# Ten of sixteen final blocks get x added in place by transfers that POOL issues, with a fourth place for the Gram copies and a new table of priorities

## The chip, the core and the metric

The kernel runs on one core of a Trainium2 chip. Five engines work side by side, each through its own list of instructions in order: TensorE (PE in the profile, with PEld for its weight loads), VectorE (DVE), ScalarE (ACT), GpSimd (POOL), and SyncE (SP), which here issues the transfers between DRAM and on-chip memory. The metric is the device time of one execution in microseconds (us); the time before is the median of 3 runs.

## The reference

x has 2048 tokens of 512 features in float32. After a layer norm, two branches are computed from the same xn and joined at the end:

```
xn = layernorm(x)
q, k, v = split_heads(xn @ wqkv)                       # 32 heads of 16
phi(t) = where(t > 0, t + 1, exp(t)) + 1e-6
kv = phi(k)^T @ v      z = sum over tokens of phi(k)   # per head
s  = (phi(q) @ kv / (phi(q) @ z + 1e-6)) @ wo
g  = silu((gelu(xn @ w_gate) * (xn @ w_up)) @ w_down)  # 512 -> 1792 -> 512
out = x + s * g
```

## The kernel before, in words

**Products.** A float32 factor is split into a high part of reduced precision and a low remainder (`split`: ACT casts the high part, DVE subtracts it). Each product is then three matmuls, high by high, high by low and low by high (`sum3`). The large products are Strassen products of two-by-two blocks, seven instead of eight (`PRODUCTS`); POOL forms sums of blocks for them, and ACT and DVE split these.

**Stages.** Tokens are worked on in blocks of 128. First x is loaded, normalized and transposed, k and q are computed, and a Gram matrix of phi(k) and xn is gathered over all tokens in four banks of PSUM, `gps`. Then comes the feed-forward branch in two passes of 1024 tokens (p = 1, then p = 0), each with units of w_gate, w_up and w_down, whose prepared forms go to DRAM in the first pass and come back in the second. The banks of gate and up products are called FX, FY, FZ, those of the down products DX, DY, DZ. The sums of the down products stand in eight tiles `acc`, for p = 1 also stored to DRAM (`g1_d`) and loaded again as `g1_0` to `g1_7` for the final stage, so that the space can be used between.

**Gram copies.** After its last matmul each `gps` bank is copied to a tile `GTa` and stored to `g_d`. Two copies are made by ACT, two by DVE. The tiles come from a ring of three places in the pool `up`, shared with other tiles of tag "p", so that the later copies wait until a store of an earlier one has landed. Places of this pool are used again by the first gate values `g` of the feed-forward branch.

**Final stage.** `s_forms` loads the normalized queries from DRAM in blocks (`pb`, `wide`) and makes the Strassen forms: Xh, Xl for p = 1, and sf0h, sf0l, sf1h, sf1l for p = 0. `s_quad(p, c, ...)` then makes seven products in four PSUM banks SX, SY, SZ, SV, and `block(dh, th, ...)` finishes each output block of 128 x 512. There are sixteen, by p, k = 2·dh + c and th. A block multiplies s by silu(g) and adds x. The way is A (product into PSUM by DVE), B (product into the g or acc tile by DVE) or C (DVE saves the sum, POOL multiplies). The add of x then is one more instruction, on POOL for the blocks in `ON_POOL` and else on DVE; it adds into a tile `xp` that `x_again` loaded with x before. SP stores the result: for p = 1 one store of 512 KB for every pair of blocks, for p = 0 one of 256 KB for every block. The very last block, `LAST`, is done in two halves.

**Layout.** s comes out with 32-column pieces of its 512 columns in another order than g. The views `turned` and `by_turn` rearrange while they read, and x and the output are laid out on the host in this turned order for all blocks.

**Order.** Nothing is written in program order. `do` records each operation with an engine and a cost, `Plan.order` plays a list scheduler over them with the numbers in `PRIORITY` (one for each operation, the smallest first among those that are ready), and each engine's list is what comes out. So a change of any number can move work on all five lists.

Of the kernel before, what the change touches and what calls it, by code (L numbers as in the profile page):

```python
# [40 lines left out]

PRIORITY = """
# [1497 lines left out]
```

## Time and profile before

| | us |
|---|---|
| three runs | 595.03, 593.09, 595.22 (median 595.03) |
| the profiled execution, own time | 594.95 |
| its span, first to last instruction | 593.0 |
| around the span | 1.95 |
| PE busy | 583.7 (98%) |
| DVE busy | 484.0 (82%) |
| POOL busy | 345.4 (58%) |
| ACT busy | 323.4 (55%) |
| mean DMA rate | 250 GB/s |

A row of the timeline gives start, duration, engine, source line, operation, tiles and count; in brackets behind it the idle time ahead and what ended it. Matmuls overlap: one of 128x512 is drawn 0.39 us long, while the next one starts 0.227 us after it. So a lost stretch of PE is the distance of two starts less 0.227, and the idle time that a row shows is some 0.16 us less than the loss. For a transfer the view of DMA issues gives the size and the median time from issue to landing.

### The profile page before, as it was taken

How to read it: one execution, taken by the hardware profiler on the slowest of the kernel's cores; microseconds unless marked ns; L12 is line 12 of the kernel's file. 1: busy time of each engine (PE TensorE's matmuls, PEld its weight loads, DVE VectorE, ACT ScalarE, POOL GpSimd, SP SyncE). 2: the span in 40 equal slices, each digit the busy share in tenths (PEclk: the TensorE clock that was granted, in tenths of full speed). 3: DMA queues.
4: the chain of work that ended last, by engine and by line, in shares of the span. 5: the costliest groups of instructions: out<-in, count | busy, mean ns of one | idle time of the engine just before them, and what ended most of it. 6: DMA issues, size and time to landing. Idle time of an engine off the chain costs nothing.

```text
span 593.0 us, 8082 instructions
## 1 busy us (share of the span) xinstructions
PE 583.7 (98%) x2588; PEld 478.7 (81%) x2588; DVE 484.0 (82%) x729; ACT 323.4 (55%) x588; POOL 345.4 (58%) x291
## 2 busy tenths in 40 slices
PE   9999999999999999999999999999999999999996
PEld 7888888887888888888888878888788888887774
DVE  6999888984788987899888975777458887779997
ACT  6766778775766654575454325434325531457741
POOL 3503586325796966879588325356335652666776
PEclk9999999999999999999999999999999999999999
DMA  7157775556958766974659999699759977899725
GB/s 253 50 177 222 239 244 157 169 177 223 355 185 273 247 208 207 341 267 160 219 175 378 374 330 342 179 321 289 266 203 360 408 260 226 264 328 340 257 109 224
DMA packets 80969, 148.37 MB, mean 250 GB/s; under 512 B 18592, under 2 KB 34208, under 8 KB 80928
## 3 DMA queue, kind: packets, MB, share of 16 engines
q1 hardware_dynamic: 80928, 147.87, 72.9%
q8 instruction: 20, 0.33, 0.2%
q14 instruction: 21, 0.17, 0.1%
HBM read 83.62 MB, written 64.23 MB: 249 GB/s over the span
## 4 chain that ended last, share of the span: by engine, by line
PE 89%; DVE 5%; DMA 4%; ACT 1%; SPq 0%; issue 0%; POOL 0%; DVEq 0%; ACTq 0%
PE FX L573 25%; PE DX L573 12%; PE FZ L573 12%; PE gps L573 7%; PE DZ L573 6%; PE FY L573 6%; PE X L573 6%; PE DY L573 3%; PE Z L573 3%; PE q L573 2%; PE k L573 2%; PE Y L573 1%; DMA w<-w_d 1%; PE SX L573 1%; DVE Xl L554 1%; DMA xp0h<-in_xt 1%
## 5 line engine op out<-in xcount | busy, mean ns | idle before, releaser
L573 PE MATMUL FX<-Xh,w 128*128 128x512 f32 x448 | 152.0, 389 | 0.4 <-DMA w<-w_d 0.4
L1140 POOL TENSOR_TENSOR h<-h,g 128x512 f32<-128x512 f32 x42 | 63.2, 1506 | 76.4 <-DVE h L554 61.1
L573 PEld LDWEIGHTS FX<-Xh,w 128*128 128x128 f32 x448 | 84.0, 188 | 18.2 <-ACT fu L548 0.8
L554 POOL TENSOR_TENSOR h<-h,h 128x512 f32<-128x512 f32 x56 | 83.5, 1490 | 19.2 <-DVE hf3l L554 4.2
L573 PE MATMUL FX<-Xl,w 128*128 128x512 f32 x224 | 87.2, 389 | 0.0
L573 PE MATMUL FZ<-Xh,w 128*128 128x512 f32 x224 | 77.4, 389 | 0.0
L548 ACT COPY fu<-FX 128x512 f32<-128x512 f32 x56 | 32.9, 588 | 57.4 <-PE FX L573 43.9
L573 PE MATMUL gps<-pks,xns 128*128 128x512 f32 x192 | 50.3, 392 | 0.0
L573 PEld LDWEIGHTS FZ<-Xh,w 128*128 128x128 f32 x224 | 42.0, 188 | 8.8
L573 PEld LDWEIGHTS FX<-Xl,w 128*128 128x128 f32 x224 | 42.0, 188 | 8.7
L554 POOL TENSOR_TENSOR wide<-wide 128x256 f32<-128x256 f32 (+1 forms) x38 | 38.6, 1027 | 14.4 <-DVE m L554 6.5
L1166 DVE TENSOR_TENSOR acc<-acc,DX 128x512 f32<-128x512 f32 x48 | 32.4, 682 | 16.0 <-PE DX L573 15.8
L573 PE MATMUL FZ<-Xl,w 128*128 128x512 f32 x112 | 43.6, 389 | 0.0
L557 POOL TENSOR_TENSOR zacc<-zacc,kp 128x512 f32<-128x512 f32 x16 | 24.6, 1536 | 30.9 <-DVE kp L849 28.0
L573 PEld LDWEIGHTS gps<-pks,xns 128*128 128x128 f32 x192 | 35.7, 188 | 7.3
L573 PE MATMUL FY<-Xh,w 128*128 128x512 f32 x112 | 39.2, 391 | 0.8 <-DVE g L554 0.8
L1132 ACT ACTIVATE g<-g 128x512 f32<-128x512 f32 x42 | 26.6, 633 | 19.9 <-DVE g L554 19.7
L554 POOL TENSOR_TENSOR wide<-q,zacc 128x512 f32<-128x512 f32 x16 | 21.3, 1354 | 21.6 <-DMA q<-q_d 12.1
L554 DVE TENSOR_TENSOR g<-fu,FZ 128x512 f32<-128x512 f32 x28 | 19.1, 682 | 15.9 <-PE FZ L573 9.1
L573 PE MATMUL X<-kq,Xh 128*128 128x512 f32 x96 | 31.2, 393 | 0.0
L548 ACT COPY fe<-FX 128x512 f32<-128x512 f32 x28 | 16.5, 588 | 26.1 <-PE FX L573 18.9
L1166 DVE TENSOR_TENSOR acc<-acc,DZ 128x512 f32<-128x512 f32 x32 | 21.7, 683 | 8.6 <-PE DZ L573 8.5
(377 smaller groups left out, 1537.7 us busy)
## 6 DMA issues: line engine op xcount, KB each, us to landing
w_d<-w SPq DMA_DIRECT2D x36, 512.0 KB, 4.7
w<-w_d SPq DMA_DIRECT2D x36, 512.0 KB, 6.2
wd_d<-wd SPq DMA_DIRECT2D x21, 512.0 KB, 4.7
wd<-wd_d SPq DMA_DIRECT2D x21, 512.0 KB, 5.6
x<-in_first SPq DMA_DIRECT2D x16, 256.0 KB, 3.0
q_d<-qp SPq DMA_DIRECT2D x16, 256.0 KB, 2.2
q<-q_d SPq DMA_DIRECT2D x16, 256.0 KB, 5.0
pn_d<-wide SPq DMA_DIRECT2D x16, 256.0 KB, 5.5
```

The costliest lines, as they stand in the source:

```text
L548: do("ACT", act(n), lambda o, i: nc.scalar.copy(o, i), dst, src, name=name)
L554: do(eng, c, lambda o, p, q: getattr(e, f"tensor_{op}")(o, p, q), dst, a, b, name=name)
L557: do("POOL", pool(D), lambda o, i: nc.gpsimd.tensor_add(o, o, i), dst, src, name=name)
L573: nc.tensor.matmul(o, v[i], v[i + 1], start=start and part == 0 and i == 0, stop=stop and part == 1 and i == len(v) - 2, skip_group_check=on)
L1132: curved("gelu", do("ACT", curve(NC), lambda o, i: nc.scalar.activation(o, i, AF.Gelu_apprx_tanh), g, ps if e is None else g, name="gelu"))
L1140: do("POOL", pool(NC), lambda o, i: nc.gpsimd.tensor_mul(o, o, i), h, g, name="h")
L1166: do("DVE", dve(NC), lambda o, i: nc.vector.tensor_add(o, o, i), a, ps, name="acc")
```

## The change

- Ten of the sixteen blocks (all eight of p = 1, and (k, th) = (0, 0) and (2, 1) of p = 0) are listed in `NATURAL`. For them the product goes into the g or acc tile (way A becomes B), and then x is added to that tile by a transfer from DRAM which accumulates, issued by POOL (`gained`). The tile is then stored from there by SP. The separate add, and the `xp` tile of p = 1 with its four loads of 512 KB, are gone; for p = 0 six loads of 256 KB take the place of four of 512 KB. The ten blocks are stored one by one, in the tile's own layout; the host lays x and the output out accordingly.
- `ON_POOL` keeps four blocks of p = 0. By the built lists DVE makes seven adds fewer and one more (block (0, 1) of the last quad, before on POOL), and POOL makes four adds fewer (two of p = 1, two of p = 0) and ten issues more.
- The Gram copies have a ring of their own with four places.
- `sf1` of p = 0 is made from tiles `pb` in places of the ring `BR` that `xp` used before, no longer from `wide`.
- All numbers of `PRIORITY` are other numbers.

```
+NATURAL = {(p, k, th) for p in range(2) for k in range(4) for th in range(2) if p or (k, th) in ((0, 0), (2, 1))}
 PRIORITY = """
-113295 113257 110076 102616 117147 119271 0 2123 110187 109121 111695 111606 111697 111790 116707 118955 118027 116257 75973 94787 75934 94720 91206
...
+173791 176819 174775 169344 169336 176625 174707 169786 173425
 """
...
+    def gained(dst, src):
+        op = do("POOL", 0.9, lambda o, i: nc.gpsimd.dma_start(o, i, accum_op=ALU.add), dst, src, name="xg")
+        op.port, op.land = False, 4.0
...
     for c in range(KT):
-        g = U("p", range(18, 21), f"GTa{c}")
+        g = U("gt", [18, 19, 20, 14], f"GTa{c}")
         copy("DVE" if c % 2 else "ACT", g, gps[c], D, "GT")
         dma(g_d(c, (slice(None), c)), g, 256, "store")
...
-    ON_POOL = ((3, 0, 1), (0, 0, 1), (1, 0, 0), (2, 0, 1), (2, 1, 0), (2, 1, 1), (3, 0, 0), (3, 1, 1))
+    ON_POOL = ((2, 0, 1), (2, 1, 0), (3, 0, 0), (3, 1, 1))
...
         def block(dh, th, e, ps, to):
-            v, o = g[dh, c, th], xp[2 * dh + c]
+            v, o = g[dh, c, th], xp.get(2 * dh + c)
             how = WAYS.get((n, dh, th), "A")
             k = 2 * dh + c
+            natural = (p, k, th) in NATURAL
+            if natural and how == "A":
+                how = "B"
...
+            if natural:
+                gained(v, ext(xt[p, k, th]))
+                dma(ext(out[k * P:(k + 1) * P, p * HALF + th * NC:][:, :NC]), v, 256, "store")
+                return
...
-                if not p:
-                    dma(ext(out[k * P:(k + 1) * P, lo:lo + w]), x, w // 2, "store")
-            if p:
-                left[k] = left.get(k, 2) - 1
-                if not left[k]:
-                    dma(ext(out[k * P:(k + 1) * P, HALF:2 * HALF]), o, 512, "store")
+                dma(ext(out[k * P:(k + 1) * P, lo:lo + w]), x, w // 2, "store")
...
-    def x_again(p):
+    def x_again():
         got = {}
-        whole = {} if p else {hl: tile_in("xf", f"{hl}0", [P, 2, HALF], F32, f"xp0{hl}", 2) for hl in "hl"}
-        for k in (0, 2, 1, 3):
-            got[k] = tile_in("dp", ring("br", BR), [P, HALF], F32, f"xp{p}{k}", 4) if p else whole["hl"[k // 2]].part(
-                [Res() for _ in range(4)], (slice(None), k % 2))
-            dma(got[k].map(lambda ap: ap.rearrange("p (h c) -> p h c", h=2)), ext(xt[p, k].rearrange("h p c -> p h c")), 512, "first")
+        for c, hl in enumerate("hl"):
+            whole = tile_in("xf", f"{hl}0", [P, 2, HALF], F32, f"xp{c}", 2)
+            for k in (c, c + 2):
+                got[k] = whole.part([Res() for _ in range(4)], (slice(None), k // 2))
+                for th in range(2):
+                    if (0, k, th) not in NATURAL:
+                        dma(got[k].part(got[k].res[2 * th:2 * th + 2], (slice(None), slice(th * NC, (th + 1) * NC))), ext(xt[0, k, th]), 256, "first")
         return got
```

How the lists move is shown at three places, by rows of the built programs: line, operation, tiles with their numbers, size, and the semaphores waited for. A semaphore named for an engine counts that engine's work. DMAHW0 to DMAHW7 count the landings of SP's transfers, which take the eight in turn; DMASW0 to DMASW7 do so for POOL's.

**The Gram copies, on DVE.** Before, at the end of the last `gps` matmuls; `w12` and `w13` are weight forms, `g11_0` is the first gate value, which frees the bank FY:

```order
L554 TENSOR_TENSOR w00_1609<-raw0_859,w00_1609 128x512 [waits Activation_49]
L554 TENSOR_TENSOR w12_1635<-w1tmp_1623,w12_1635 128x512 [waits Activation_49]
L554 TENSOR_TENSOR w13_1651<-w1tmp_1623,w13_1651 128x512 [waits Activation_49]
L550 COPY GTa3_1672<-gps3_435 128x512 [waits DMAHW6_49,DMAHW1_49,PE_49]
L554 TENSOR_TENSOR g11_0_1680<-fe1_0_1658,FY0_1617 128x512 [waits DMAHW5_49,DMAHW2_49,Activation_49]
L554 TENSOR_TENSOR wd00_1668<-wide_206,wd00_1668 128x512 [waits Activation_49]
```

and now:

```order
L555 TENSOR_TENSOR w00_1609<-raw0_859,w00_1609 128x512 [waits Activation_49]
L551 COPY GTa1_1627<-gps1_382 128x512 [waits DMAHW5_49,PE_49]
L555 TENSOR_TENSOR w12_1643<-w1tmp_1622,w12_1643 128x512 [waits Activation_49]
L555 TENSOR_TENSOR w13_1654<-w1tmp_1622,w13_1654 128x512 [waits Activation_49]
L551 COPY GTa3_1672<-gps3_379 128x512 [waits DVE_49,PE_49]
L555 TENSOR_TENSOR g11_0_1684<-fe1_0_1676,FY0_1634 128x512 [waits DMAHW0_49,DVE_49,Activation_49]
L555 TENSOR_TENSOR wd00_1665<-wide_206,wd00_1665 128x512
```

The copy of `gps1` stands ahead of `w12` now, and the copy of `gps3` waits for no transfer; `g11_0` waits for DMAHW0, on which the store of `GTa1` lands.

**Loads of weights in the second pass, on SP.** Before (`g1_d` rows store acc tiles, `w100` and `w102` are gate weights of the next unit):

```order
L523 DMA g1_d_92<-acc1_5_2006 128x512 [waits DMAHW3_49,DVE_49]
L523 DMA wd53_3514<-wd53_d_165 128x1024 [waits DMAHW4_49,PE_49]
L523 DMA wd63_3520<-wd63_d_169 128x1024 [waits DMAHW5_49,PE_49]
L523 DMA g1_d_92<-acc1_3_1983 128x512 [waits DMAHW6_49,DVE_49]
L523 DMA g1_d_92<-acc1_1_1977 128x512 [waits DMAHW7_49,DVE_49]
L523 DMA g1_d_92<-acc1_7_2019 128x512 [waits DMAHW0_49,DVE_49]
L523 DMA w100_3538<-w100_d_154 128x1024 [waits DMAHW1_49,PE_49]
L523 DMA w102_3550<-w102_d_156 128x1024 [waits DMAHW2_49,PE_49]
```

and now:

```order
L524 DMA g1_d_92<-acc1_1_1967 128x512 [waits DMAHW3_49,DVE_49]
L524 DMA wd53_3513<-wd53_d_165 128x1024 [waits DMAHW4_49,PE_49]
L524 DMA g1_d_92<-acc1_3_2002 128x512 [waits DMAHW5_49,DVE_49]
L524 DMA w102_3522<-w102_d_156 128x1024 [waits DMAHW6_49,PE_49]
L524 DMA wd63_3530<-wd63_d_169 128x1024 [waits DMAHW7_49,PE_49]
L524 DMA g1_d_92<-acc1_5_1998 128x512 [waits DMAHW0_49,DVE_49]
L524 DMA w100_3543<-w100_d_154 128x1024 [waits DMAHW1_49,PE_49]
L524 DMA g1_d_92<-acc1_7_2023 128x512 [waits DMAHW2_49,DVE_49]
```

`w102` stands ahead of two of the stores of acc tiles now, `w100` ahead of one.

**The final stage, on POOL and DVE.** POOL before, from the first sum for the forms of p = 0 to the first add of p = 0:

```order
L554 TENSOR_TENSOR pb000_5290<-pb001_5349,pb000_5290 128x512 [waits DMAHW3_49,Pool_49]
L554 TENSOR_TENSOR g1_2_5263<-g1_2_5263,se1_1_5423 128x4x4x32 [waits DVE_49]
L554 TENSOR_TENSOR pb001_5349<-pb001_5349,pb000_5290 128x512 [waits DVE_49,Activation_49,Pool_49]
L554 TENSOR_TENSOR pb001_5349<-pb001_5349 128x512 [waits DMAHW4_49,Pool_49]
L554 TENSOR_TENSOR wide_206<-wide_206 128x512 [waits DMAHW6_49,DMAHW0_49,DVE_49]
L554 TENSOR_TENSOR wide_206<-wide_206 128x512 [waits DMAHW7_49,Pool_49]
L554 TENSOR_TENSOR wide_206<-wide_206 128x512 [waits Pool_49]
L554 TENSOR_TENSOR wide_206<-wide_206 128x512 [waits DMAHW5_49,Pool_49]
L554 TENSOR_TENSOR xp11_5175<-xp11_5175,g1_2_5263 128x512 [waits DMAHW2_49]
L554 TENSOR_TENSOR xp10_5269<-xp10_5269,g1_1_5255 128x512 [waits DVE_49]
L554 TENSOR_TENSOR acc0_2_3688<-acc0_2_3688,se1_3_5560 128x4x4x32 [waits DVE_49]
L554 TENSOR_TENSOR xp0h_5408<-xp0h_5408,acc0_2_3688 128x512 [waits DMAHW3_49,PE_49,Pool_49]
```

and now; the rows of line 561 are the new issues:

```order
L555 TENSOR_TENSOR g1_2_5260<-g1_2_5260,se1_1_5375 128x4x4x32 [waits DVE_49]
L561 DMA g1_2_5260<-in_xt 128x512 [waits Pool_49]
L555 TENSOR_TENSOR pb001_5314<-pb001_5314,pb000_5267 128x512 [waits DVE_49,PE_49]
L561 DMA g1_5_5140<-in_xt 128x512 [waits DVE_49]
L555 TENSOR_TENSOR pb010_5176<-pb010_5176 128x512 [waits DMAHW6_49,DVE_49]
L555 TENSOR_TENSOR pb010_5176<-pb011_5217,pb010_5176 128x512 [waits Pool_49]
L555 TENSOR_TENSOR pb011_5217<-pb011_5217,pb010_5176 128x512 [waits DVE_49,Pool_49]
L561 DMA g1_4_5099<-in_xt 128x512 [waits DVE_49]
L561 DMA g1_1_5251<-in_xt 128x512 [waits DVE_49]
L555 TENSOR_TENSOR pb011_5217<-pb011_5217 128x512 [waits DMAHW0_49,Pool_49]
L561 DMA g1_7_5187<-in_xt 128x512 [waits DVE_49]
L555 TENSOR_TENSOR pb001_5314<-pb001_5314 128x512 [waits DMAHW4_49]
```

Five issues stand ahead of the last sum (`pb001`). Each waits for the product that DVE writes into the tile. Behind these rows follow four issues, the product of `acc0_2`, the tenth issue (`acc0_5`) and four adds.

The end of DVE's list before:

```order
L554 TENSOR_TENSOR SZ3_5577<-su2_3_5607,SZ3_5577 128x512 [waits PE_49]
L554 TENSOR_TENSOR acc0_3_3776<-acc0_3_3776,SZ3_5577 128x4x4x32 [waits DVE_49]
L554 TENSOR_TENSOR SX3_5544<-acc0_6_3851,SX3_5544 128x256 [waits PE_49]
L554 TENSOR_TENSOR xp0l_5425<-xp0l_5425,SX3_5544 128x256 [waits DMAHW4_49,DVE_49]
L554 TENSOR_TENSOR SX3_5544<-acc0_6_3851,SX3_5544 128x256 [waits DVE_49]
L554 TENSOR_TENSOR xp0l_5425<-xp0l_5425,SX3_5544 128x256 [waits DVE_49]
```

and now:

```order
L555 TENSOR_TENSOR acc0_3_3784<-acc0_3_3784,SZ3_5577 128x4x4x32 [waits DVE_49]
L555 TENSOR_TENSOR SX3_5536<-acc0_6_3849,SX3_5536 128x256 [waits PE_49]
L555 TENSOR_TENSOR xp1_5399<-xp1_5399,acc0_3_3784 128x512 [waits DMAHW0_49,DVE_49]
L555 TENSOR_TENSOR SX3_5536<-acc0_6_3849,SX3_5536 128x256 [waits DVE_49]
L555 TENSOR_TENSOR xp1_5399<-xp1_5399,SX3_5536 128x256 [waits DMAHW2_49,DVE_49]
L555 TENSOR_TENSOR xp1_5399<-xp1_5399,SX3_5536 128x256
```

The add of block `acc0_3`, on POOL before, stands between the two halves of the last block.

More of the change, by code (lines that the diff above doesn't have):

```diff
@@ L1430, in block @@
                 tt("POOL" if (n, dh, th) in ON_POOL else "DVE", "add", by_turn(x), by_turn(x), rs[h], w, "xr")
-                if not p:
-                    dma(ext(out[k * P:(k + 1) * P, lo:lo + w]), x, w // 2, "store")
-            if p:
-                left[k] = left.get(k, 2) - 1
-                if not left[k]:
-                    dma(ext(out[k * P:(k + 1) * P, HALF:2 * HALF]), o, 512, "store")
-        left = {}
+                dma(ext(out[k * P:(k + 1) * P, lo:lo + w]), x, w // 2, "store")
         prod_s(X, 1, True)
@@ L1466, in s_quad @@
         block(0, 1, u2, Z, Z)
-    def x_again(p):
+    def x_again():
         got = {}
-        whole = {} if p else {hl: tile_in("xf", f"{hl}0", [P, 2, HALF], F32, f"xp0{hl}", 2) for hl in "hl"}
-        for k in (0, 2, 1, 3):
-            got[k] = tile_in("dp", ring("br", BR), [P, HALF], F32, f"xp{p}{k}", 4) if p else whole["hl"[k // 2]].part(
-                [Res() for _ in range(4)], (slice(None), k % 2))
-            dma(got[k].map(lambda ap: ap.rearrange("p (h c) -> p h c", h=2)), ext(xt[p, k].rearrange("h p c -> p h c")), 512, "first")
+        for c, hl in enumerate("hl"):
[5 more added lines that the diff above has]
+                        dma(got[k].part(got[k].res[2 * th:2 * th + 2], (slice(None), slice(th * NC, (th + 1) * NC))), ext(xt[0, k, th]), 256, "first")
         return got
-    forms, gg, xps = {}, {}, {}
+    forms, gg = {}, {}
     for p in (1, 0):
@@ L1488 @@
             gg[p] = {key: acc[0, key] for key in KEYS}
-        xps[p] = x_again(p)
+        xp = {} if p else x_again()
         for c in range(2):
-            s_quad(p, c, forms[p], gg[p], xps[p])
+            s_quad(p, c, forms[p], gg[p], xp)
     in_turn([("S", 0, 1, 3), ("S", 0, 1, 4)])
@@ L1495, with by_blocks @@
         o.fn()
+def by_blocks(v, turn):
+    import numpy as np
+    got = np.empty_like(v)
+    for at in np.ndindex(*v.shape[:3]):
+        got[at] = v[at] if at in NATURAL else turn(v[at])
+    return got
 def laid_out(inputs, shape):
@@ L1513, in laid_out @@
         "in_first": np.stack([piece(v) for v in FIRST]),
-        "in_xt": x.T.reshape(d // P, P, 2, 2, 4, 4, -1).transpose(2, 0, 3, 1, 5, 4, 6).reshape(2, d // P, 2, P, -1),
+        "in_xt": by_blocks(x.T.reshape(d // P, P, 2, 2, -1).transpose(2, 0, 3, 1, 4),
+                           lambda b: b.reshape(P, 4, 4, -1).transpose(0, 2, 1, 3).reshape(b.shape)),
         "in_wo": wo,
@@ L1537 @@
     r = _run(nc, [arrays], core_ids=[0])
-    y = r.results[0]["out_y"].reshape(shape[-1], 2, 2, 4, 4, -1).transpose(1, 2, 4, 3, 5, 0)
-    return _np.ascontiguousarray(y).reshape(shape)
+    y = by_blocks(r.results[0]["out_y"].reshape(shape[-1] // P, P, 2, 2, -1).transpose(2, 0, 3, 1, 4),
+                  lambda b: b.reshape(P, 4, 4, -1).transpose(0, 2, 1, 3).reshape(b.shape))
+    return _np.ascontiguousarray(y.transpose(0, 2, 4, 1, 3)).reshape(shape)
```

292 rows, old and new, of the table PRIORITY are left out of this document.

## The prediction

> **What bounds the kernel now.** I read the page's chain first, then busy time by stretches, then PE's own timeline around each stretch that is not full.
>
> ```profile
> PE 89%; DVE 5%; DMA 4%; ACT 1%; SPq 0%; issue 0%; POOL 0%; DVEq 0%; ACTq 0%
> ...
> 0.00:20.00 20.00, 18.55 (x90) 15.76 (x91) 15.24 (x37) 14.24 (x29) 6.50 (x12) 1.00 0.64 211
> 20.00:100.00 80.00, 79.98 (x364) 65.46 (x363) 75.33 (x136) 59.02 (x107) 39.76 (x37) 1.00 0.61 186
> 100.00:300.00 200.00, 199.16 (x878) 164.26 (x877) 165.01 (x225) 121.74 (x226) 135.14 (x121) 1.00 0.68 233
> 300.00:480.00 180.00, 179.62 (x801) 147.49 (x800) 134.06 (x193) 76.97 (x139) 97.72 (x76) 1.00 0.86 304
> ...
> 551.00:561.00 10.00, 9.61 (x43) 7.49 (x42) 10.00 (x15) 9.12 (x18) 7.20 (x5) 1.00 0.62 198
> 561.00:571.00 10.00, 10.00 (x46) 8.29 (x45) 9.96 (x17) 5.06 (x10) 8.26 (x7) 1.00 0.44 163
> 571.00:581.00 10.00, 9.50 (x39) 6.73 (x38) 10.00 (x16) 2.90 (x6) 5.67 (x4) 1.00 0.51 202
> 581.00:588.00 7.00, 6.31 (x28) 4.88 (x26) 6.54 (x12) 0.82 (x2) 6.84 (x7) 1.00 0.53 198
> ```
>
> The columns are PE, PEld, DVE, ACT and POOL busy, clock, DMA share and GB/s. PE carries 89% of the chain and is full almost everywhere: it lacks 0.84 us in 100 to 300, 0.38 in 300 to 480, 0.39 and 0.50 in the final stage. The edit adds no matmul and takes none, so these gaps, the first 20 us and the end after the last matmul are all that it can move. DVE is full from 551 to 581 (10.00, 9.96 and 10.00 of 10 us): the final stage has two engines at their limit.
>
> The gaps themselves, in PE's timeline:
>
> ```profile
> 143.94 0.39 PE L573 MATMUL FX<-Xh,w 128*128 128x512 f32 x1
> 145.15 0.70 PE L573 MATMUL FY<-Xh,w 128*128 128x512 f32 x2 [0.82 <-DVE g L554]
> ...
> 353.58 0.39 PE L573 MATMUL DX<-hf6h,wd 128*128 128x512 f32 x1
> 354.35 0.71 PE L573 MATMUL FX<-Xh,w 128*128 128x512 f32 x2 [0.38 <-DMA w<-w_d]
> ...
> 557.52 0.39 PE L573 MATMUL SX<-Xh,ms 128*128 128x512 f32 x1
> 558.30 0.73 PE L573 MATMUL SX<-Xh,ms 128*128 128x512 f32 x2 [0.39 <-ACT se L548]
> ...
> 573.49 0.40 PE L573 MATMUL SX<-sf0h,ms 128*128 128x512 f32 x1
> 574.06 0.50 PE L573 MATMUL SX<-sf1l,ms 128*128 128x512 f32 x1 [0.17 <-DVE sf1l L554]
> ...
> 575.78 0.39 PE L573 MATMUL SX<-sf1h,ms 128*128 128x512 f32 x1
> 576.45 0.50 PE L573 MATMUL SZ<-sf0h,ms 128*128 128x512 f32 x1 [0.28 <-DVE xp L554]
> ...
> 586.92 0.39 PE L573 MATMUL SX<-sf1h,ms 128*128 128x512 f32 x1
> ```
>
> A loss is the distance of starts less 0.227, and about 0.1 more because the first matmul after a gap is drawn that much longer (0.50 against 0.39; a pair 0.70 against 0.61). That gives 0.98 + 0.09 = 1.07 at 144, 0.54 + 0.08 = 0.62 at 354, 0.55 + 0.11 = 0.66 at 558, 0.34 + 0.11 = 0.45 at 574 and 0.44 + 0.11 = 0.55 at 576: 3.35 us in all. This is what better cover can win. PE ends at 587.31; the span ends at 593.0.
>
> **The change, part by part.**
>
> *Gram copies.* The first gap:
>
> ```profile
> 135.50 0.69 DVE L554 TENSOR_TENSOR w<-raw,w 128x512 fp32r<-128x512 f32 x1 [0.42 <-ACT w L548]
> ...
> 139.64 1.21 SPq L523 DMA_DIRECT2D g_d<-GTa  x2
> ...
> 143.72 0.69 DVE L550 COPY GTa<-gps 128x512 f32<-128x512 f32 x1 [2.53 <-DMA g_d<-GTa]
> 144.33 0.68 DVE L554 TENSOR_TENSOR g<-fe,FY 128x512 f32<-128x512 f32 x1
> ...
> DMA to landing us min/median/max: 3.8/4.0/6.2
> ```
>
> DVE waits 2.53 us for a GTa store before its third copy, and g, which frees FY for PE, is queued behind that copy. With four places no copy waits for another's store. By the new list g waits instead for the store of GTa1. Its bank is done nine matmuls earlier than the last one, by count of the rows at about 136.9; the copy follows the w row of 135.50, its store goes out near 137.9, and 4.0 later, at 141.9, it has landed. FX, which g's other input is saved from, ends by the same count near 141.5, so g runs from 142.1. PE asks for FY near 144.2. So the whole 1.07 goes, unless that store takes over 5.3 us (of the four, the slowest took 6.2). Taken: -1.07; ends 0 and -1.07.
>
> *Weight loads in the second pass.*
>
> ```profile
> 343.99 2.08 SPq L523 DMA_DIRECT2D g_d<-acc  x3
> ...
> 346.16 8.05 DMA w<-w_d
> ```
>
> The load that PE missed at 354 was issued behind three stores of acc tiles that SP held from 343.99 to 346.07. In the new list w102 stands ahead of two of them and w100 ahead of one. One store less ahead is about 0.7 us, more than the gap of 0.54. Taken: -0.62; ends 0 and -0.62, with the load's 8.05 us (the median for this kind is 6.2) as the doubt.
>
> *Adds on DVE.* Seven go, one comes back.
>
> ```profile
> 568.38 0.59 DVE xp L554
> ...
> 575.80 0.61 DVE xp L554
> ```
>
> These two pieces of the chain of waits show adds of x on the path itself, 0.60 us from start to start. Six of the seven lie before 577, so DVE has 6 x 0.60 = 3.6 us of room where it had none. The gap at 574 is a low part that DVE made late, the one at 576 a bank that an add held until it had read it; with way B the product itself frees the bank. Both go: 0.45 + 0.55 = -1.00. The gap at 558 is ACT's, which had casts to do, and nothing takes work from ACT; I leave it. Ends: 0 (PE finds another late part) and -1.66 (all three).
>
> *POOL.* Four adds leave, ten issues come. No POOL issue is in this trace. The nearest rows:
>
> ```profile
> 582.56 0.33 SPq L523 DMA_DIRECT2D out_y<-xp0h  x1
> ...
> 547.10 1.75 POOL L554 TENSOR_TENSOR wide<-wide,pb 128x512 f32<-128x512 f32 x1
> ...
> 572.16 3.00 POOL L554 TENSOR_TENSOR xp<-xp,g 128x512 f32<-128x512 f32 x2
> ```
>
> An SP issue of the same size takes 0.33, the slowest POOL instruction of this size 1.75. It is an issue, but of software on POOL rather than of SP, so I take 1.0, between. POOL is busy 7.20 + 8.26 + 5.67 + 6.84 = 27.97 of the 37 us from 551 to 588: 9.03 idle. The adds free 3.00 for the pair of p = 1 and some 2.6 for the two of p = 0, so 14.6 us hold ten issues up to 1.46 each. Covered at 1.0; cost 0, from 0 to 17.5 - 14.6 = +2.9.
>
> *Transfers.* The loads of xp, 4 x 512 KB, leave a time when DMA is loaded and come back as ten reads of 256 KB spread over the final stage at a share of 0.44 to 0.62. Before, no store of p = 1 waited for a transfer; now each does, and SP's queue holds those behind it. Only the last counts, acc0_5, with five stores behind it at the end. How long it takes is bounded by
>
> ```profile
> out_y<-xp0h SPq DMA_DIRECT2D x4, 256.0 KB, 2.1
> ...
> wide<-pn_d SPq DMA_DIRECT2D x8, 256.0 KB, 4.0
> ...
> xp0h<-in_xt SPq DMA_DIRECT2D x2, 512.0 KB, 7.0
> ...
> 581.12 0.67 DVE L554 TENSOR_TENSOR acc<-acc,SV 128x512 f32<-128x512 f32 x1
> ```
>
> Its product ends at 581.8 in this trace, and with fewer adds ahead no later against PE. Its store may go out until about 587.6 without pushing those behind: 5.8 us for issue and landing. I take 1.0 + 4.0 (a load of the same size from DRAM in this stage): covered by 0.8. Worst, 1.75 + 7.0: +2.95.
>
> *The end.* One add of 512 columns, 0.60, now stands on DVE between the halves of the last block, but POOL's last add, whose store went out at 588.90 ahead of the last two, is gone.
>
> ```profile
> 588.74 0.42 DVE L554 TENSOR_TENSOR xp0l<-xp0l,SX 128x256 f32<-128x256 f32 x1
> ...
> 588.90 0.33 SPq L523 DMA_DIRECT2D out_y<-xp0h  x1
> 589.33 0.88 SPq L523 DMA_DIRECT2D out_y<-xp0l  x2
> ```
>
> DVE's last add then starts near 589.3 and the last store near 589.8, where the second of the pair starts now (589.33 + 0.44). Cost 0, within 0.3.
>
> *Sum* against the profiled execution's own time: 594.95 - 1.07 - 0.62 - 1.00 = 592.26. The median of the runs is 595.03, 0.08 higher; I say 592.3.
>
> **A rule against the change.** The DVE rows of the final stage are TENSOR_TENSOR (those at 581.12 and 588.74 stand for them), and they follow each other every 0.60 us. The Trainium skill (SBUF — State Buffer, "A bandwidth-pool intuition that's wrong" and "Who interferes with whom") says that POOL writes the descriptors of its own transfers into SBUF and cannot do so while DVE holds the port pair that both share; a transfer of 620 ns took 3100 ns under a DVE copy. The page also says that a tensor_tensor takes only the read side of that pair, so by that the trace's rows speak for no stall. No run here shows it yet; what it would do stands in rival 2.
>
> **Rivals.**
> 1. *The stall moves within the final stage.* DVE stays full, and a late form shows at another product. For it: DVE at 10.00 with ACT at 9.12 in 551 to 561. Only Gram and weights pay: 593.3. Chance 0.20.
> 2. *POOL becomes the bound.* The sums for the forms of p = 0 stand behind five issues in POOL's list, and each issue waits for a DVE product. It decides from 1.46 us per issue. At 1.75 the stage is 2.9 longer and its 1.00 is not won: 594.95 - 1.69 + 2.9 = 596.2; each further 0.1 costs 1.0, and from 1.93 it is slower by more than 0.5%. If an issue also had to wait out three DVE instructions at 0.60, it would last 1.0 + 1.8 = 2.8, and the time would be 593.26 + 28 - 14.6 = 606.7. (That last case is how the rule above would come out.) For it: nothing in the trace prices an issue, and DVE is full. Against it: an idle POOL, and four adds gone. Chance 0.13, of it 0.03 with the DVE wait.
> 3. *The last in-place store holds SP.* Up to +2.95: 595.2. Chance 0.08.
> 4. *The Gram edit wins nothing*, since g waits for another store: 593.3. Against it: 1.3 us of slack. Chance 0.07.
> 5. *All gaps close*, those of 558 and 571 too: 594.95 - 3.35 - 0.3 = 591.3. Chance 0.12.
>
> **How the numbers follow.** The forecast has 0.40. A new order can also make new small waits, and the runs before lie 2.1 us apart, so each case spreads by about 1 us; 0.5%, about what a measurement here tells from no change, is 3.0 us, and faster than 592.05 takes half of the forecast, all of rival 5 and a little of 1 and 4: 0.35. Slower than 598.0 is most of rival 2: 0.10. The rest is 0.55. The range runs from 589.9 (all gaps closed, and the lower mode of the runs) to 596.4 (rival 2 at the bound of its row); the forecast's own is 591.0 to 593.6.
>
> **What would show it.** No wait of DVE for GTa, no gap at FY near 144. No wait of FX for w near 354. In the final stage DVE under 9.5 of 10, no PE wait for sf1l or for a product's add, the issues of POOL near 1 us and ended before the last sum is needed. Between the last matmul and the end 5.7 us as now. I am wrong if POOL waits show in front of ACT's casts of sf0h, if SP waits for an accumulating transfer at the end, or if PE shows new gaps in stages that the edit only reorders.

## The result, and the profile after

| | before | after |
|---|---|---|
| median of the runs, us | 593.91 (592.50 to 595.22, 6 runs) | 597.81 (597.15 to 599.50, 6 runs) |
| ratio to before, 95% interval | | 1.0068 [1.0047, 1.0089] |
| profiled execution, its span | 594.95, 593.0 | 597.15, 595.3 |
| PE's last matmul ends | 587.31 | 587.31 |
| from there to the end of the span | 5.69 | 7.99 |

The changed kernel is slower by 3.9 us by the medians; 592.3 was forecast. The two profiled executions are 2.2 us apart: the one of before lies 1.0 above its median, the one of after 0.7 below. The traces explain these 2.2 us; the runs below serve for the rest.

The chain of after:

```profile
PE 88%; DVE 6%; DMA 3%; issue 1%; POOL 1%; ACT 0%; SPq 0%; DVEq 0%; ACTq 0%; POOLq 0%
```

Its busy time by stretches, in the columns of the prediction (PE, PEld, DVE, ACT, POOL busy, clock, DMA share, GB/s):

```profile
100.00:300.00 200.00, 200.00 (x883) 165.49 (x883) 167.85 (x227) 121.72 (x227) 140.36 (x123) 1.00 0.67 235
300.00:360.00 60.00, 60.00 (x266) 49.67 (x266) 49.28 (x75) 25.16 (x46) 32.34 (x25) 1.00 0.90 328
360.00:551.00 191.00, 189.59 (x839) 154.10 (x838) 139.08 (x203) 83.67 (x147) 102.50 (x77) 1.00 0.83 284
551.00:561.00 10.00, 10.00 (x46) 8.29 (x45) 8.33 (x12) 9.28 (x18) 7.62 (x6) 1.00 0.46 153
561.00:571.00 10.00, 10.00 (x45) 8.29 (x45) 9.66 (x15) 5.87 (x11) 8.99 (x9) 1.00 0.52 111
571.00:581.00 10.00, 9.01 (x39) 6.94 (x39) 9.81 (x13) 3.28 (x6) 6.74 (x8) 1.00 0.98 184
581.00:588.00 7.00, 6.31 (x28) 4.88 (x26) 5.32 (x10) 0.59 (x2) 6.65 (x7) 1.00 1.09 263
588.00:596.00 8.00, 0.00 (x0) 0.00 (x0) 2.69 (x4) 0.00 (x0) 1.04 (x1) 0.78 0.70 261
```

PE is full from 100 to 360 now. From 360 to 551 it lacks 1.41 us of busy time and does 13 matmuls fewer in the same stretch, 839 against 852 (13 x 0.227 = 2.95 us), where before it lacked nothing:

```profile
360.00:551.00 191.00, 191.00 (x852) 156.94 (x851) 142.16 (x204) 86.45 (x153) 101.78 (x78) 1.00 0.86 290
```

(This row is of before.) And the DMA, half idle in the final stage before, is full from 571 to 588 and moves no more: 184 GB/s at a share of 0.98 from 571 to 581, where before 202 took 0.51. (The share adds up the time of the packets, so it can pass 1 where they overlap.) Setting the start of PE's n-th matmul in one trace against the n-th in the other gives the sum: +0.08 at the start, -1.11 at Gram, -1.02 from there to 360, +2.96 from 360 to 542, -0.91 in the final stage, together 0.00; then +2.30 behind the last matmul and -0.10 around the span: +2.20 (594.95 to 597.15).

DVE at Gram after, then the largest of the new waits of PE:

```profile
140.91 0.68 DVE L551 COPY GTa<-gps 128x512 f32<-128x512 f32 x1
142.34 0.69 DVE L555 TENSOR_TENSOR g<-fe,FY 128x512 f32<-128x512 f32 x1 [0.76 <-ACT fe L549]
...
530.58 6.49 POOL L555 TENSOR_TENSOR h<-h,h 128x512 f32<-128x512 f32 x4
...
536.43 1.18 DVE L555 TENSOR_TENSOR hf0l<-h,hf0h 128x512 fp32r<-128x512 f32 x1
537.54 0.67 DVE L1171 TENSOR_TENSOR acc<-acc,DZ 128x512 f32<-128x512 f32 x1
538.26 0.51 PE L578 MATMUL DZ<-hf1h,wd 128*128 128x512 f32 x1 [0.87 <-DVE acc L1171]
...
570.66 1.96 POOL L555 TENSOR_TENSOR pb<-pb 128x512 f32<-128x512 f32 x1
570.71 2.47 DVE L555 TENSOR_TENSOR sf1l<-pb,sf1h 128x512 fp32r<-128x512 f32 x1
573.70 0.68 DVE L555 TENSOR_TENSOR SY<-se,SY 128x512 f32<-128x512 f32 x1
575.13 0.50 PE L578 MATMUL SX<-sf0h,ms 128*128 128x512 f32 x1 [0.99 <-ACT se L549]
```

The third copy's wait for a store is gone, and `g` runs at 142.34. The other rows show a pattern. `hf0l` starts at 536.43 with two inputs in SBUF, while POOL is at work, and ends at 537.61, 0.54 after POOL's 537.07. `sf1l` ends at 573.18, 0.56 after POOL's 572.62. A PSUM row behind each of them (`acc`, `SY`) then frees PE's bank or feeds ACT's copy too late. The smaller new waits at 492, 515 and 532 show the same rows: the DVE row with two SBUF inputs ahead of them ends at 491.82, 515.38 and 532.42, 0.54 to 0.55 after a row of POOL (491.27, 514.84, 531.87). I call such a row locked below.

The end of after, POOL's, DVE's and SP's rows of the timeline:

```profile
578.38 0.87 POOL L561 DMA_DIRECT2D acc<-in_xt  x1 [0.63 <-DVE sf0l L555]
580.60 0.87 POOL L561 DMA_DIRECT2D g<-in_xt  x1 [1.35 <-issue]
583.14 0.88 POOL L561 DMA_DIRECT2D acc<-in_xt  x1 [0.35 <-DVE SZ L555]
583.75 5.29 POOL L555 TENSOR_TENSOR xp<-xp,acc 128x512 f32<-128x512 f32 x4
...
587.69 1.90 DVE L555 TENSOR_TENSOR xp<-xp,acc 128x512 f32<-128x512 f32 x1
...
588.73 0.33 SPq L524 DMA_DIRECT2D out_y<-acc  x1
589.15 2.80 SPq L524 DMA_DIRECT2D out_y<-xp  x5
```

Its transfers, by size and median us from issue to landing:

```profile
g<-in_xt POOLq DMA_DIRECT2D x8, 256.0 KB, 5.4
out_y<-g SPq DMA_DIRECT2D x8, 256.0 KB, 4.2
out_y<-xp SPq DMA_DIRECT2D x5, 256.0 KB, 3.5
```

The issue of acc0_5 stands at 583.14 instead of 581.8, its store at 588.73, and the issues of five stores behind it last until 591.95; before, the last one ended at 590.21 (589.33 + 0.88). Stores of 256 KB land in 3.5 to 4.2 us by the medians; before it was 2.1. The later issues, 1.74 us, and the longer landing are the 2.3 us of the tail.

### The profile page after: what moved, and what is told of

Its sections match the earlier page's. It is cut to its first block, busy times and chain, and to the rows that moved or that the text cites. A ratio compares the mean times of both kernels' runs of the same rounds, so it can differ in the third digit from the quotient of the medians.

```text
span 595.3 us, 8071 instructions
## 1 busy us (share of the span) xinstructions
PE 582.4 (98%) x2588; PEld 478.1 (80%) x2588; DVE 482.4 (81%) x723; ACT 322.7 (54%) x588; POOL 352.4 (59%) x297
## 4 chain that ended last, share of the span: by engine, by line
PE 88%; DVE 6%; DMA 3%; issue 1%; POOL 1%; ACT 0%; SPq 0%; DVEq 0%; ACTq 0%; POOLq 0%
PE FX L578 23%; PE FZ L578 12%; PE DX L578 12%; PE gps L578 7%; PE FY L578 6%; PE X L578 6%; PE DZ L578 5%; PE Z L578 3%; PE DY L578 3%; PE SX L578 2%; PE k L578 2%; PE q L578 2%; DMA q<-q_d 2%; PE Y L578 1%; PE SZ L578 1%; PE SY L578 1%
## 5 line engine op out<-in xcount | busy, mean ns | idle before, releaser
L555 POOL TENSOR_TENSOR h<-h,h 128x512 f32<-128x512 f32 x56 | 86.2, 1539 | 17.1 <-DVE hf2l L555 4.6
L555 POOL TENSOR_TENSOR wide<-wide 128x256 f32<-128x256 f32 (+1 forms) x34 | 32.0, 951 | 15.7 <-issue 6.6
L1171 DVE TENSOR_TENSOR acc<-acc,DZ 128x512 f32<-128x512 f32 x32 | 21.6, 682 | 11.2 <-PE DZ L578 8.3
L555 DVE TENSOR_TENSOR h<-fu,FZ 128x512 f32<-128x512 f32 x28 | 19.1, 682 | 10.6 <-PE FZ L578 6.3
```

The source lines that it names most:

```text
L555: do(eng, c, lambda o, p, q: getattr(e, f"tensor_{op}")(o, p, q), dst, a, b, name=name)
L1171: do("DVE", dve(NC), lambda o, i: nc.vector.tensor_add(o, o, i), a, ps, name="acc")
```

## The experiments

All runs. The ratio is to runs of before on the same chip; the last columns are of the profiled execution: end of PE's last matmul, end of the span, and the distance (the tail).

| run | median | ratio, 95% | PE ends | span | tail |
|---|---|---|---|---|---|
| e1 Gram ring alone | 599.21 | 1.0101 [1.0083, 1.0120] | 592.81 | 598.5 | 5.7 |
| e2 new order, old end | 595.89 | 1.0056 [1.0034, 1.0077] | 588.12 | 593.8 | 5.7 |
| e3 old order, new end | 604.82 | 1.0197 [1.0177, 1.0216] | 593.81 | 602.3 | 8.5 |
| e4 only p = 1 in place | 596.77 | 1.0055 [1.0040, 1.0071] | 589.69 | 595.0 | 5.3 |
| e5 (the changed kernel again) | 596.83 | 1.0072 [1.0060, 1.0084] | 587.41 | 594.9 | 7.5 |
| e6 last add on POOL | 597.80 | 1.0081 [1.0067, 1.0096] | 586.85 | 594.0 | 7.2 |
| e7 plain copies | 597.83 | 1.0090 [1.0075, 1.0106] | 590.61 | 596.0 | 5.4 |
| e8 more descriptor room | 598.20 | 1.0092 [1.0079, 1.0105] | 589.67 | 596.3 | 6.6 |
| e9 before again | 594.2 | one run | 586.58 | 592.3 | 5.7 |
| e10 new order to 360, then old | 591.83 | 0.9975 [0.9959, 0.9992] | 583.81 | 589.5 | 5.7 |
| e11 form behind products | 597.59 | 1.0074 [1.0057, 1.0091] | 587.84 | 595.2 | 7.4 |
| e12 store really last | 597.11 | 1.0060 [1.0040, 1.0080] | 587.88 | 596.0 | 8.1 |
| e13 e10 with ten in place | 597.44 | 1.0077 [1.0064, 1.0090] | 584.19 | 595.3 | 11.1 |
| e14 e10 with eight in place | 595.07 | 1.0036 [1.0022, 1.0051] | 585.14 | 592.6 | 7.5 |
| e15 locked add last | 597.15 | 1.0064 [1.0049, 1.0079] | 587.55 | 595.3 | 7.8 |
| e16 e10 again | 591.64 | 0.9975 [0.9963, 0.9986] | 583.86 | 589.6 | 5.7 |
| e17 e13 with plain copies | 592.69 | 0.9990 [0.9980, 1.0001] | 585.12 | 591.0 | 5.9 |
| e18 e13 without the transfers | 591.93 | 0.9980 [0.9965, 0.9995] | 584.89 | 590.6 | 5.7 |

### The order, in pieces

**e1, the ring alone** (the list of before is written out, so that nothing else moves).

```
-        g = U("p", range(18, 21), f"GTa{c}")
+        g = U("gt", [18, 19, 20, 14], f"GTa{c}")
```

> The kernel before with the ring of four Gram copies and nothing else; every list as before, except that the fourth copy and its store stand ahead of the first gate value. Theory (the gap at 144 is DVE's wait for a GTa store, and the ring removes it): PE's loss of 1.07 us at FY near 144 is gone, nothing else moves, 593.9 - 1.1 = 592.8 us. Rival (g waits for another store, or PE finds the next late bank): the gap stays or moves, 593.9 us.

Neither: the gap grew. DVE and PE of this run, then its busy time by stretches (the clock is the third column from the end):

```profile
141.48 1.29 DVE L655 COPY GTa<-gps 128x512 f32<-128x512 f32 x2 [0.47 <-PE gps L678]
148.00 0.69 DVE L659 TENSOR_TENSOR g<-fe,FY 128x512 f32<-128x512 f32 x1 [5.22 <-DMA g_d<-GTa]
148.83 1.19 PE L678 MATMUL FY<-Xh,w 128*128 128x512 f32 x2 [4.66 <-DVE g L659]
```

```profile
148.00:155.00 7.00, 6.17 (x15) 4.91 (x16) 3.23 (x6) 1.79 (x4) 2.27 (x3) 0.51 0.71 231
155.00:160.00 5.00, 5.00 (x24) 4.10 (x23) 2.59 (x5) 3.42 (x7) 2.28 (x3) 1.00 0.50 201
```

With four places `g` takes the place of GTa1, and in the old list GTa1 is copied just ahead of `g`: `g` waits 5.22 us for that store. In the changed kernel GTa1 is copied at 137.19, four microseconds earlier. So the ring wins nothing by itself; the ring and the copy's new place together do.

**e2 and e3, front and end exchanged.** In e1 to e4, e6, e10, e13, e14 and e16 to e18 the order in which the operations are emitted is written out:

```
-    for o in plan.order():
-        o.fn()
+    for o in sorted(plan.ops, key=lambda o: rank[o.n]):
+        emit(o)
```

`rank` comes from the two kernels' own lists, for e2 and e3 cut at the first operation of the final stage; `emit` does missing predecessors first.

> Everything up to the last down products in the order of the changed kernel, with its ring of four; the final stage as before, with x loaded and added by DVE and POOL, no transfer in place. Theory T (the whole of the +2.3 us of the profile lies behind the last matmul and comes from the final stage's new edits): the tail after the last matmul is 5.7 us again; PE comes to the final stage 0.9 us later than before, because the new order wins 1.7 us at Gram and weights and loses 2.6 at small stalls near 393, 492, 515 and 532 to 538; so 594.8 us. Rival O (the order of the earlier stages is what costs the 3.9 us of the medians): 596 us or more.

> Everything up to the last down products in the order of before, with the ring of four; the final stage as in the changed kernel, ten blocks in place. Theory T: PE comes to the final stage 1.1 us earlier than before (the ring), the final stage closes its gaps at 558, 574 and 576 (-1.7) and makes one of 1.3, and the tail is 8.0 us instead of 5.7 (+2.3): 593.9 - 1.1 - 0.4 + 2.3 = 594.7 us by the profile's terms. Rival O: without the new order of the earlier stages the loss is gone, 592.4 us.

e2 costs 2.8 us with no transfer in place and a tail of 5.7: most of the loss is there without the in-place edit. The tail is as theory T has it, the time is just under rival O's 596. e3 ran into e1's wait (143.4, 4.8 us) and tells only that its tail is 8.5.

**e9 and e10.**

> The kernel before once more, for a second profile: its profiled execution lies 1 to 2 us above the other executions of the same kernel (594.95 against medians of 593.0 to 593.9). Theory: a single wait that a run may have or not (a load of weights near 354, the start) accounts for it, and PE reaches the final stage 1 to 2 us earlier than in the first profile, the end after the last matmul again 5.7 us: 593.0 us. Rival: the differences lie in the end.

The wait for weights at 354 is absent in this second profile of before, the gaps near 574 and 576 are there again; tail 5.7.

> The new order and the ring of four up to the first weights of the second pass (about 360 us), from there the order and the final stage of before, no transfer in place. The lists coincide in what is done at that place, so that nothing is moved across it. Theory (the new order wins up to 360 us, 1.07 at Gram, 0.3 at 293 and 0.6 at the weights near 354, and loses 2.6 from 393 to 538): what it wins is kept, 1.1 to 2.0 us less than before, 591 to 592 us from 593.0. Rival (each order has its own late waits, and what is won is given back behind the seam): 593 us, no change.

e10, and e16 again, are 0.25% faster than before and the fastest here. From 360 to 551 PE is full, and the final stage, with the rows of before, has only the gap at 555:

```profile
360.00:551.00 191.00, 191.00 (x852) 156.97 (x851) 142.83 (x207) 87.17 (x156) 102.84 (x78) 1.00 0.84 289
...
571.00:581.00 10.00, 10.00 (x46) 8.11 (x45) 9.81 (x17) 2.94 (x5) 7.26 (x6) 1.00 0.60 236
```

e2 and e10 have the same code, and their lists differ between 356 and 553 alone: 1.0056 against 0.9975, some 4.8 us. So the new table, with the ring, wins 0.25% early and loses 0.8% in the second pass.

### The end, on the changed kernel

**e5 and e12, the store of acc0_5 to the end of SP's list.**

```
+    todo.append(todo.pop(todo.index(plan.ops[3032])))     # e5; operation 3032 is that store
...
+    held = todo.pop(todo.index(plan.ops[3032]))           # e12
...
+    tc.keep_in_program_order(held.fn())                   # e12, behind all others
```

> The changed kernel with one row moved: the store of acc0_5, which waits for its transfer in place until 588.7, is the last on SP instead of ahead of five others. Theory A (that store holds SP's last five): they go out as their adds end, the last one of them at 591.3 only because DVE ends at 590.7, so 0.4 us at most is won by the row alone, and 0.9 if the DMA is freer by then: 597 to 597.4 us. If SP's hold is the whole of the tail's +2.3, 595.5 us. Rival B (DVE's last adds set the end): 597.8 us, no change, with the store of acc0_5 adding one more issue at the end (+0.4).

In e5 the built list came out as the changed kernel's, so it is a second measurement of that one.

> The changed kernel with the store of acc0_5 as the very last row of SP, held there (in the run with that edit before, the list came out as the changed kernel's, so it was a second run of that one). Theory A (the store holds SP's last five until 588): the stores of the adds go out as these end; the last of them waits for DVE until 591, so 0 to 0.9 us are won: 596 to 597 us, and up to 2.3 us if the hold is the whole tail. Rival B (DVE and POOL at the end set it): no change against 596.8 to 597.8, or 0.4 more for one issue behind.

In e12 the seven stores of xp take SP from 587.61 to 592.14 all the same, and the time is that of e5 within the intervals. So the hold of that one store does not set the end by itself. It is not the only one: the store of a g tile, in place too, goes out at 587.18 ahead of the seven, and DVE's last add ends at 591.21 (590.46 + 0.75).

**e6, e15 and e11, DVE's locked instructions.** e6 puts (3, 0, 1) back into `ON_POOL`; e15 and e11 move DVE rows:

```
 SX3<-acc0_6,SX3 128x256          e15
-xp1<-xp1,acc0_3 128x512
 SX3<-acc0_6,SX3 128x256
 xp1<-xp1,SX3 128x256 x2
+xp1<-xp1,acc0_3 128x512

-sf1l<-pb011,sf1h 128x512         e11
 SZ<-su,SZ 128x512
 SY<-se,SY 128x512
+sf1l<-pb011,sf1h 128x512
```

> The changed kernel with the add of block (0, 1) of the last quad on POOL, as before, instead of on DVE; all else as it is. Theory B (DVE's 1.90 us set the end): DVE ends near 589.2 instead of 590.7; POOL, busy until 589.0 with four adds, does a fifth until 590.3, and its store goes out near 590.5 ahead of two more: last store start 591.3 to 590.9, 0 to 0.5 us won, since POOL is late itself. Theory A (SP held until 588.73 and a loaded DMA): 0 to 0.4 won. Together with a fall of the DVE add's 1.90: if POOL's adds no longer run beside it they take 1.27 each as before.

> The changed kernel with DVE's add of block (0, 1), xp1 and acc0_3, both in SBUF, and its store behind the last two halves instead of between them. Theory L (this add waits for POOL's last add at 589.0 and holds the second half behind it; products and adds of the halves have a PSUM input and do not wait): both halves are done near 589.1, the add ends 0.56 us after POOL, near 589.6, the last store goes out near 590.1 to 590.5 instead of 591.3: 1 us won, 596.2 to 596.8 us. Rival A (SP's hold and a full DMA set the end): tail as it was, 597 to 597.8 us.

> The changed kernel with one row moved on DVE: the low part sf1l of 570.71, two inputs in SBUF, stands behind the two PSUM instructions SZ and SY that followed it, not ahead of them. Theory L (a DVE instruction with two SBUF inputs that meets a running POOL instruction waits until POOL's is over and then takes 0.56 us; with a PSUM input it does not wait): SY ends near 572 instead of 574.4, PE's gap of 1.15 us near 574 is gone, and the low part still ends 0.56 after a POOL row's end; PE ends about 1.1 us earlier, but the tail behind the last matmul, set by transfers and POOL, may keep part: 596.0 to 597.2 us. Rival (the DVE instruction is slow from its own operands, or PE waits for another): the gap stays, 597 to 597.8 us.

Neither e6 nor e15 is faster than the changed kernel (e6's profile ends 1.3 us earlier, its median does not show it). Both move DVE's locked add, which ends at 589.59 in the changed kernel, and leave what else stands near it, SP's held store at 588.73 and POOL's last add at 589.04. No run moves all three, so how they share the end is not shown. In e11 DVE does what theory L says:

```profile
571.28 0.69 DVE L555 TENSOR_TENSOR SZ<-su,SZ 128x512 f32<-128x512 f32 x1 [0.67 <-PE SZ L578]
571.88 0.69 DVE L555 TENSOR_TENSOR SY<-se,SY 128x512 f32<-128x512 f32 x1
572.48 3.26 DVE L555 TENSOR_TENSOR sf1l<-pb,sf1h 128x512 fp32r<-128x512 f32 x2
...
572.32 2.27 POOL L555 TENSOR_TENSOR pb<-pb 128x512 f32<-128x512 f32 x1
...
575.20 0.50 PE L578 MATMUL SX<-sf1l,ms 128*128 128x512 f32 x1 [1.69 <-DVE sf1l L555]
```

The PSUM rows pass beside POOL in 0.69, and the low part is late instead. PE then waits for that: a gap of 1.85 in place of 1.15. The lock is real, but moving one row moves the wait.

**e4, e7, e8.** e4 leaves p = 0 out of `NATURAL` and gives one of the two adds to POOL, the other to DVE; e7 takes `accum_op` off (product left out in ten blocks); e8 sets `dynamic_dma_scratch_size` to 1280.

> The changed kernel with only the eight blocks of p = 1 in place; the two blocks of p = 0 are loaded and added as before (one on DVE, one on POOL), all lists else as they are. Theory A (the two late transfers in place set the end: they load the DMA until 589 and hold SP's last stores): the tail goes from 8.0 back to about 6 us, 2 us less than the changed kernel, 595.8 us. Rival B (DVE's added instruction of 1.90 us between the halves of the last block sets the end, beside POOL's adds that are late): the tail stays at 7.5 to 8 us, 597.5 us or more, since DVE and POOL have one add more each.

> The changed kernel with the ten transfers of POOL as plain copies of x into the tile, without accumulating (the product of those ten blocks is left out of the output); issue, bytes, lists and waits are the same. Theory C (the accumulation itself makes the transfers slow and keeps the DMA full, 0.98 to 1.09 from 571 to 588, so that stores land in 3.5 to 4.2 us instead of 2.1): the transfers of POOL take half the DMA time, land in under 4 us instead of 5.5, the share falls to about 0.7, acc0_5's store goes out by 587, and 1 to 2 us are won: 596 us. Rival (256 KB more traffic of any kind, or DVE and POOL at the end): no change, 597.8 us.

> The changed kernel with 1280 bytes in place of 1024 per partition for the descriptors of POOL's transfers. Theory D (POOL's issue of g1_0 idles 1.35 us until 580.6 because three transfers fill that room, and issues of 1.57 and 1.32 us are longer for the same cause): the idle time before it is gone, the issue of acc0_5 moves from 583.1 to about 581.8, POOL's four adds start 1.3 earlier, and the tail is 0.5 to 1.3 shorter: 596.5 to 597.3 us. Rival (the wait is something else): all as in the changed kernel, 597.8 us.

All three shorten the tail (5.3, 5.4, 6.6), and in all three PE ends 2 to 3 us later, part of it behind a new locked row of DVE (579.67, 2.11 us in e4; 581.04, 2.27 in e7; 579.53, 2.83 in e8), so that little or nothing is won. Matmul by matmul, 0.7 to 1.2 us of it come before 551, where these edits change nothing, and 1.6 to 2.1 in the final stage. So on the changed kernel itself no run shows the time falling when the accumulation goes. In e8 the idle time of 1.35 ahead of the issue is gone, as theory D says; but POOL's next row then meets `sf1l`, which lasts 2.83, and PE waits 1.25. That left open what the tail is made of.

### The transfers in place, on a full PE

e10 has PE full and a tail of 5.7. e13 and e14 put blocks in place into it; e17 copies without accumulating, e18 leaves the transfers out.

```
-        op = do("POOL", 0.9, lambda o, i: nc.gpsimd.dma_start(o, i, accum_op=ALU.add), dst, src, name="xg")
+        op = do("POOL", 0.9, lambda o, i: nc.gpsimd.dma_start(o, i), dst, src, name="xg")     # e17
+        op = do("POOL", 0.9, lambda o, i: None, dst, src, name="xg")                          # e18
```

> The kernel with the new order up to 360 us and the old one behind it, but with the ten blocks in place: each issue stands on POOL where the add stood, each store on SP behind it; the seven adds leave DVE, the last block (0, 1) stays on POOL. Theory T (the transfers in place cost the end 2 us whatever the order: DMA full, POOL late with its last adds): tail 7 to 8 us instead of 5.7, 1.5 to 2.5 us more than that kernel without them, 593.3 to 594.3 us. Rival O (the order alone is what cost, transfers in place are free or win): 591 to 592 us, as that kernel or less.

> The same with only the eight blocks of p = 1 in place, whose transfers end by 582; p = 0 is loaded and added as before. Theory T (only the two late ones hold the end): tail 5.3 to 5.7 us, 591 to 592 us, as the kernel without transfers in place, or 0.5 less if DVE's room closes the gap at 558. Rival (eight issues and adds that meet on POOL and DVE make new waits in the final stage, as in the changed kernel near 574): 593 us or more.

> The kernel with the new order up to 360 us and the old one behind it, once more, as the base for the two runs with transfers in place: 0.25% less than the kernel before, 591.5 to 592 us, if the first measurement holds.

> The ten blocks in place on the old order behind 360 us, but the ten transfers copy x into the tile without accumulating (the product of these blocks is left out of the output); issues, bytes, waits and lists are the same. Theory C (an accumulating transfer takes the DMA 1.6 us of all 16 engines where a plain one takes 0.7 to 0.95, and lands in 5.0 to 5.5 us instead of 3.3; so the DMA is full from 571 to 593 and the last stores queue in it): the end comes down from 595.3 to 591 or 592 us, time 592.5 to 594 us instead of 597.4. Rival (each block waits in a row for product, issue, transfer and store, and SP takes them in order, whatever the rate): no more than 1 us is won, 596.4 us or more.

> The same kernel with the ten transfers left out (x is missing in these ten blocks of the output); the products go in place and the sixteen stores go out one by one as before. Theory C: with nothing that accumulates, the DMA has gaps again and the end stands 5.7 us behind the last matmul, 589.5 us or earlier, time 591 to 592 us. Rival (sixteen single stores, six pieces of loads and POOL's four adds are themselves what fills the end): tail over 7 us, 594 us or more.

PE ends at 584.2 in e13, 3.1 us earlier than in the changed kernel, and the span ends at 595.3 in both. The DMA of 571 to 596, by queue (packets, MB, share of 16 engines; q0 is POOL's), in e13 and then in e17:

```profile
q0 software_dynamic: 1008, 1.84, 44.8%
q1 hardware_dynamic: 2160, 3.67, 41.4%
...
g<-in_xt POOLq DMA_DIRECT2D x5, 256.0 KB, 5.8
```

```profile
q1 hardware_dynamic: 2160, 3.67, 40.1%
q0 software_dynamic: 560, 1.84, 20.9%
```

The same 1.84 MB take packets of 44.8% of 25 us, 11.2 us of all 16 engines, when they accumulate, and 5.2 when they copy, 6.0 us less. The tail falls from 11.1 to 5.9 and the median by 4.75 us (by 0.87% when each is taken against before on its own chip); without the transfers the tail is 5.7. So the accumulation makes the tail of e13. How it does so, by rows of e13 and then of e17:

```profile
571.00:581.00 10.00, 10.00 (x45) 8.15 (x45) 8.52 (x15) 3.14 (x6) 5.72 (x7) 1.00 0.92 191
581.00:588.00 7.00, 3.19 (x15) 2.29 (x13) 4.54 (x9) 0.00 (x0) 7.00 (x7) 1.00 0.99 236
...
582.87 5.59 POOL L660 TENSOR_TENSOR xp<-xp,acc 128x512 f32<-128x512 f32 x4
585.61 0.42 DVE L660 TENSOR_TENSOR xp<-xp,SX 128x256 f32<-128x256 f32 x1
588.40 0.33 SPq L629 DMA_DIRECT2D out_y<-acc  x1
588.83 3.07 SPq L629 DMA_DIRECT2D out_y<-xp  x5
```

```profile
571.00:581.00 10.00, 10.00 (x45) 8.12 (x44) 8.51 (x14) 3.08 (x6) 7.11 (x10) 1.00 0.83 300
...
584.31 0.40 SPq L629 DMA_DIRECT2D out_y<-acc  x1
584.80 3.28 SPq L629 DMA_DIRECT2D out_y<-xp  x5
```

The DMA is full at 191 to 236 GB/s, and the store of acc0_5, which waits for its transfer in place, goes out at 588.40 instead of 584.31. The adds of the five stores behind it are done by 586.03 on DVE and 588.46 on POOL, but these stores go out after it, from 588.8 to 591.9, and land in 2.8 to 3.8 us. So here the last transfer in place does hold SP, as rival 3 of the prediction has it. Theory C stands as far as the accumulation is the cause, and DVE's lock is not what ends e13. Not separated is how much comes by way of POOL: with plain copies its issues are shorter too, and its last add ends 1.6 us behind PE's last matmul instead of 4.3.

Eight in place (e14) cost 3.4 us, where theory T had them cost nothing. No transfer in place is left at its end; POOL's last add ends 2.8 us behind PE's last matmul, against 1.6 in e10, and PE itself ends 1.3 us later.

The two losses do not add. In the profiles with ten accumulations the spans end at 594.0 to 596.3, whether PE ends at 584.2 or 589.7 (only in e3, where PE itself ends at 593.8, is it later). Behind PE's late order of the changed kernel only 2.3 us of it show; on e10's order 5.4.

## Why the prediction was wrong, step by step

The profiled execution took 4.89 us more than the sum, 597.15 for 592.26. Two things that the sum put at nothing failed: the new order lost 2.96 us of PE from 360 to 542, and the tail grew by 2.30. The three gains that it priced came about as large as forecast (-1.11, -1.02, -0.91 for -1.07, -0.62, -1.00), though not all by the way that was given.

- *Gram copies, -1.07:* measured -1.11 in the trace, by the mechanism given. Rival 4 was real, as e1 shows: the ring without the earlier copy makes `g` wait 5.22 us.
- *Weights, -0.62:* the gap at 354 is gone, but the second profile of before does not have it either. A wait that one execution had was sized as a gain.
- *Adds on DVE, -1.00:* the gaps at 574 and 576 are gone, and a wait of 1.15 + 0.11 at 574 has come: rival 1. e10 has those gaps closed with the adds still on DVE.
- *POOL, 0:* right for the changed kernel. Issues took 0.86 to 1.57 us, POOL's last add ended 1.73 us behind PE's last matmul (before 1.57), and rival 2 is out. But POOL idled 1.35 us ahead of one issue, and the issue of acc0_5, behind it and behind POOL's product of acc0_2, came at 583.14, some 1.4 us after DVE had finished that tile (by 581.03 + 0.68).
- *Transfers, 0:* a failed step. An accumulating read was priced as a load of its size, "1.0 + 4.0" from 581.8, and only its latency was weighed, for acc0_5 alone. The issue came at 583.14, and the store went out 5.59 us later, at 588.73, past the 587.6 that would have been free. The medians of landing are 5.4 to 5.8 us, and the DMA's time was left out: 1.6 us of all 16 engines for 256 KB against 0.75 (11.2 and 5.2 over seven transfers), in a stage that also stores 4 MB. Rival 3's hold of SP is real, in e13 above all, but its cause was not weighed, and moving that one store in the changed kernel won nothing (e12).
- *The end, 0 within 0.3:* 2.30, as far as e13 and e17 show from the same cause. DVE's added instruction lasted 1.90 rather than 0.60, since it waited out POOL's adds (589.04 + 0.55 = 589.59), but moving it alone won nothing (e15).
- *Missing from the sum, the other failed step:* the new order itself. "A new order can also make new small waits" was given 1 us of spread; it lost 2.96 us of PE from 360 to 542, in stages that the edit only reorders, and 4.8 us between e2 and e10. At 492, 515, 532, 537 and 574 the rows show DVE's lock ahead of PE's wait; at 393 they do not. Only the one at 574 was tried (e11), so for the others the lock is read from the rows and not shown by a run.
- *The base:* 594.95 is near the top of before's runs; 593.0 to 593.9 would have been nearer.

The rule that was weighed did not matter here: the longest issue took 1.57 us, not 2.8. Another sentence of that page does: the Trainium skill (SBUF — State Buffer, "Who interferes with whom") says that a DVE instruction with two SBUF inputs contends with a POOL instruction that reads SBUF, that one of them blocks fully, and that one with at most one SBUF input, outside the faster two-port modes, is free. The rows agree, 0.54 to 0.56 us after POOL's end each time, and 0.69 for the PSUM rows.

What stays open: how the held store, POOL and DVE share the end of the changed kernel; how much of the accumulation's cost comes by way of POOL's longer issues; and how much of before's own spread, 592 to 595 us, is which gap.

## What to carry to other kernels

A transfer that adds on its way costs more than a copy of its size: price it by the share of the DMA that it fills, not only by its latency, and see what else that stage has to move. A re-searched order is an edit of its own; compare it alone, in pieces, at places where both orders have done the same work, and keep the piece that wins (e10: 0.25% faster than before). A gap in one profiled execution is a candidate for a gain, not a gain, until a second profile has it too.

## What was not expected of the hardware

- An accumulating transfer of 256 KB takes 144 packets, whose time beside other traffic adds up to 1.6 us of all 16 DMA engines; the plain one 80 packets and 0.75 us (1008 and 560 packets over seven). POOL's issue of it takes 0.86 to 0.88 us at the least, a plain one 0.54 to 0.58.
- POOL idles ahead of an issue (1.35 us from 579.25 in the changed kernel) with a room for descriptors of 1024 bytes a partition, and not at 1280 (e8, one profile).
- After 4.66 us without a matmul PE was granted half its clock (0.51 from 148 to 155 in e1; matmuls 0.427 us apart instead of 0.227), and some 13 matmuls later the full one. The wait of 4.82 us and the slow matmuls cost 7.7 us against e10, which has neither. The Trainium skill (TensorE: Matmul & The Clock Gate, "Part 1: The HAM clock gate") puts the idle time from which this happens at about 3.4 us; the gaps of 1.15 us in the changed kernel showed no drop (clock 1.00 from 571 to 581).
